# First block of the first MLP in two parts, with the second block between them; seven tiles of weights converted during the second block

## The chip, the cores and the metric

One core of a Trainium2 chip runs the whole kernel. The metric is the device time of one execution in microseconds (us). The matmul engine is TensorE (PE in the profile; PEld is its weight loads), VectorE is DVE, ScalarE is ACT, GpSimd is POOL, and SyncE (SP) issues all DMAs. TensorE's clock has two levels, 2.4 GHz and 1.2 GHz; the profile gives the granted share.

## The reference, cut to what matters

A linear attention with a decaying state feeds two MLPs, all in float32:

```python
# attention: q, k, v, alpha of shape (4, 8, 768, 48)
for t in range(S):
    state = alpha[:, :, t, :, None] * state + k[:, :, t] (outer) v[:, :, t]
    y[:, :, t] = q[:, :, t] @ state
x = y as (3072 tokens, 384)
h = x @ w1_in;  x1 = (h * sigmoid(1.702 * h)) @ w1_out      # d_ff 2048
h = x1 @ w2_in; out = (h - tanh(h)) @ w2_out                # d_ff 2048
```

## The kernel before

**MLPs.** The 3072 tokens are six blocks of 512 (`L1`, `L2`). A *step* is one block with one of 16 tiles `m` of 128 hidden units. `gemm1` makes the hidden tile (nine matmuls of 128x512: three parts of d_model times three products of high and low halves), `sig_1` the activation (ACT tanh at L387, then DVE at L388 into `gf`), `g_split` its high half on ACT (`ghi`, L391) and low half (`glo`, L392) on DVE or POOL, and `gemm2` (nine matmuls) adds the tile's share to three accumulator banks. `gemm2` runs `LAG = 3` steps behind `gemm1`. The hidden tile has two banks by turns (`HB[s % 2]`), so `gemm1` of step s waits for `sig_1` of step s-2. There are 192 steps; steps 0 to 15 are the first block, 16 to 31 the second. At the end of a block `evac` scales the banks into `xs` and stores them to `x1t` in DRAM.

**Weights** come as float64 and are converted by `conv`, which works on three tiles at a time: `w_split` of the oldest (`whi` on ACT at L191, `wlo` on DVE at L192), `w_join` of the next (DVE, L174), `w_bits` of a third (DVE, L161 and L162). Before the steps `conv` runs five times, which leaves tiles 0 to 2 done, 3 joined and 4 started; then it runs once in each step of the first block (13 of these 16 calls have work). The float buffers are three `cf` tiles and, for the first MLP, two more inside `xs`.

**Attention** goes by chunks g of 128 tokens, four to a block, six to a batch row; chunks 0 to 3 are done before step 0. The steps of a block make the next block's chunks: in the first block one chunk in three steps. A chunk's work: `prep(g, 0)` and `prep(g, 1)` are two scans (DVE, L241; the first with a reciprocal), `prep(g, 2)` two multiplications (L247, L248; DVE for chunks below 8, then POOL), `prep(g, 3)` is `a_guard` (ACT, L252), which squares the scans' results in place; `a_scores(g, 0)` and `a_scores(g, 1)` are matmuls (L277) into banks 5 and 6, copied out by ACT (L282, L290) and masked by POOL (L287) for chunks below 8; `a_out` makes the output (L306, L313) and the state's increment (L322); `a_state` (DVE, L333, L334) needs the scan of chunk g+1; `a_evac` copies the output out, `a_done` stores it, loads chunk g+2 and (`a_back`) brings the output back with d_model on the partitions; `a_x` splits it into `xhi` (ACT, L363) and `xlo`.

**Order.** From `begin` to the end of step 15, `in_order` chains the instructions of each engine's queue in the order in which the code issues them. An instruction there waits behind all that stands before it on its engine. After that a planner sets the order. The names above have their lines below; these few set the order inside a step of the first block:

```python
gemm1(i, m, h, n)
conv(1); fetch()                       # one tile further; its next load
g_split(*prev)
attend(4 + r // 4, r % 4)              # r by m: scores, scores, output
sig_1(s, h, n)
a_done, a_state at m % 3 == 2; prep(.., 3) a step later
gemm2(m, s - LAG, acc, n)
```

Of the kernel before, what the change touches and what calls it, by code (L numbers as in the profile page):

```python
# [17 lines left out]
C = 128  # L18
# [4 lines left out]
NP = H // 2  # L23
DP = 112
NB = 512
L1 = [(t, 512) for t in range(0, NTOK, 512)]
L2 = [(t, 512) for t in range(0, NTOK, 512)]
KT = DM // 128
# [40 lines left out]
def linear_attention_mlps(ctx, tc, xq, xv, fa, fv, cst, w1, w2, out):  # L69
# [49 lines left out]
    for _ in range(2):  # L119
# [22 lines left out]
    x1t = dr.tile([KT, 128, NTOK], F32, name="x1t")  # L142
    xt = dr.tile([H, D, NTOK], F32, name="xt")

    cfs = {
        1: cf + [xsf[:, i * WC : (i + 1) * WC] for i in range(2)],
        2: cf + f_c,
    }


    wsrc = {1: w1, 2: w2}
# [186 lines left out]
    def a_evac(g, b):  # L338
        ys = ysb[g % 2 if g < FULL else 0]
        for hh in range(2):  # L340
            A.copy(ys[:DP, 2 * C * hh : 2 * C * hh + 2 * C], bank[b + hh][:DP, : 2 * C])
        y4 = ys.rearrange("p (b a t) -> p b a t", b=2, a=2)
        tk = slice(g * C, g * C + C)
        for n in range(2):
            for hh in range(2):
                SP.dma_start(out=xt[2 * n + hh :: 4, :, tk].rearrange("h d t -> d h t"), in_=y4[64 * n : 64 * n + D, hh])  # L346
        if g >= FULL:
            a_back(g)
            a_x(g)


    def a_at(g):
        j = max(j for j, (t, _) in enumerate(L1) if t <= g * C)
        return xhi[j % 2], xlo[j % 2], slice(g * C - L1[j][0], g * C - L1[j][0] + C)

    def a_back(g):
        _, xl, o = a_at(g)
# [7 lines left out]


    def gemm1(i, m, h, n):
        xh, xl = xhi[i % 2], xlo[i % 2]
        c = 0
        for k in range(KT):  # L370
            ws = slice(k * 128, (k + 1) * 128)
            for w, x in ((whi, xh), (whi, xl), (wlo, xh)):
                P.matmul(out=h, lhsT=w[m][:, ws], rhs=x[:, k, :n], start=c == 0, stop=c == 3 * KT - 1)  # L373
                c += 1

    def gemm2(m, s, acc, n):
        for k in range(KT):
            ws = slice(DM + k * 128, DM + (k + 1) * 128)
            for c, (w, x) in enumerate(((whi, ghi), (wlo, ghi), (whi, glo))):
                P.matmul(out=acc[k][:, :n], lhsT=w[m][:, ws], rhs=x[s % 3][:, :n], start=m == 0 and c == 0,  # L380
                         stop=m == MT - 1 and c == 2)

    HB = [bank[3], bank[4]]

# [33 lines left out]
    def tanh_2(s):  # L418
        V.copy_predicated(gf[s % 2], f_m[0], f_d[0])

    def evac(l, t0, n, acc):
        for k in range(KT):
            if k == 1:
                V.tensor_scalar(out=xs[:, k, :n], in0=acc[k][:, :n], scalar1=0.5 if l == 1 else 1.0, scalar2=None,
                                op0=ALU.mult)
            else:
                A.activation(out=xs[:, k, :n], in_=acc[k][:, :n], func=AF.Copy, scale=0.5 if l == 1 else 1.0)
            if l == 2:
                SP.dma_start(out=out[k, :, t0 : t0 + n], in_=xs[:, k, :n])
        if l == 1:  # L430
            SP.dma_start(out=x1t[:, :, t0 : t0 + n].rearrange("k p t -> p k t"), in_=xs[:, :, :n])
# [3 lines left out]
        SP.dma_start(out=xr, in_=x1t[:, :, t0 : t0 + n].rearrange("k p t -> p k t"))  # L435

    def x1_split(j, k):
        i = (len(L1) + j) % 2
        A.copy(xhi[i][:, k], xr[:, k])  # L439
        G.tensor_tensor(out=xlo[i][:, k], in0=xr[:, k], in1=xhi[i][:, k].bitcast(F32), op=ALU.subtract)  # L440


    LAG = 3
# [113 lines left out]
    prep(4, 2)  # L557
    prep(4, 3)

    steps = [(1, j, m) for j in range(len(L1)) for m in range(MT)] + [(2, j, m) for j in range(len(L2)) for m in range(MT)]  # L560
    NS, NS1 = len(steps), len(L1) * MT

    def place(s):
# [2 lines left out]
        t0, n = (L1 if l == 1 else L2)[j]  # L566
        alt = i >= len(L1) - 1 and (i - len(L1)) % 2
        return l, j, m, i, t0, n, [bank[b] for b in ((5, 6, 7) if alt else (0, 1, 2))]

    for s in range(NS + LAG):  # L570
        if s:
# [3 lines left out]
        if s < NS:  # L575
            l, j, m, i, t0, n, acc = place(s)
            h = HB[s % 2][:, :n]
            gemm1(i, m, h, n)
            if l == 1 and j:
                sig_1(s, h, n)  # L580
            elif l == 1:
                conv(1)
                fetch()
            if l == 2:
# [3 lines left out]
        if s == NS:  # L588
            u_flag()
        if s < NS:  # L590
            if l == 1 and j + 1 < len(L1):
                t1, n1 = L1[j + 1]
                if j:
                    parts, span = n1 // C * 4, 11
                    todo = range(min(parts, -(-m * parts // span)), min(parts, -(-(m + 1) * parts // span)))
                else:
                    todo = ((4 * (m // 3) + m % 3,) if m % 3 < 2 else (4 * (m // 3) + 2, 4 * (m // 3) + 3)) if m < 12 else ()
                for r in todo:
                    attend(t1 // C + r // 4, r % 4)
            if l == 1 and j == 0:  # L600
                sig_1(s, h, n)
                if m % 3 == 2 and m < 12:
                    a_done(m // 3 + 4)
                    a_state(m // 3 + 4)
                if m % 3 == 0 and 0 < m < 13:
                    prep(m // 3 + 4, 3)
                if m % 3 == 1 and m > 3:
                    a_x(m // 3 + 3)
            if 2 <= j < 4 and m % 2:
                w_check(l, 8 * (j - 2) + m // 2)  # L610
            if 2 <= j < 4 and not m % 2:
# [22 lines left out]
                        x1_split(j + 1, m - 6)  # L634
        if s >= LAG:
            l, j, m, i, t0, n, acc = place(s - LAG)
            gemm2(m, s - LAG, acc, n)
            if m == MT - 1:
                evac(l, t0, n, acc)
        if s == MT - 1:  # L640
            in_order(begin)


# [103 lines left out]
```

## Time and profile before

| | us |
|---|---|
| median of 3 runs (lowest to highest) | 963.45 (963.1 to 965.75) |
| profiled execution, device time | 968.22 |
| its span, first to last instruction | 966.2 |
| TensorE busy in the span | 924.4 (96%) |
| DVE busy | 611.3 (63%) |
| ACT busy | 458.5 (47%) |
| POOL busy | 191.5 (20%) |

The span is what the trace covers; the device time has 2.0 us more around it. The profiled execution is 4.8 us longer than the median of the runs. Shares over the whole span mix stages: the 48 us before the first step, the first block, the blocks with attention beside them, and the rest.

### The profile page before, as it was taken

Reading aid. Unit: us, or ns where it says so; the run is one execution under the profiler, and the core shown is the slowest. Engines: PE = TensorE matmul, PEld = TensorE weight load, DVE = VectorE, ACT = ScalarE, POOL = GpSimd, SP = SyncE. Lnnn points to the kernel's source line nnn. Section 1 sums busy time; section 2 is a strip of 40 time slices with the busy share of each in tenths; the row PEclk is TensorE's granted clock in tenths of the full one; section 3 lists DMA queues with packets and bytes.
Section 4 is the critical chain, followed back from the end, with each engine's and each line's share of the span. In section 5 each row is a group of like instructions: output and inputs, shape, how many; then the busy total and the mean of one; then the engine's idle time right before and its main releaser. Section 6 shows DMA issues by size and latency. Waiting matters only on the chain.

```text
span 966.2 us, 13208 instructions
## 1 busy us (share of the span) xinstructions
PE 924.4 (96%) x4870; PEld 728.8 (75%) x4870; DVE 611.3 (63%) x916; ACT 458.5 (47%) x969; POOL 191.5 (20%) x150
## 2 busy tenths in 40 slices
PE   5579999999999999999999999999999999999997
PEld 4357777777777777777788888888888888888885
DVE  7799982442444453643249996776777777766663
ACT  4445534333444534333344564555555665545542
POOL 1201213453444444343320200100100101000000
PEclk9989999999999999999999999999999999999999
DMA  9767533231465443751224330100323430000001
GB/s 254 229 186 234 159 83 96 73 106 63 138 194 190 139 143 104 267 170 46 87 67 163 130 131 1 66 33 1 98 99 98 165 98 0 34 1 1 33 1 37
DMA packets 58042, 101.84 MB, mean 105 GB/s; under 512 B 4992, under 2 KB 37376, under 8 KB 57968
## 3 DMA queue, kind: packets, MB, share of 16 engines
q1 hardware_dynamic: 57968, 100.90, 33.1%
q8 instruction: 40, 0.66, 0.3%
q14 instruction: 34, 0.28, 0.1%
HBM read 86.73 MB, written 14.16 MB: 104 GB/s over the span
## 4 chain that ended last, share of the span: by engine, by line
PE 83%; DVE 7%; DMA 4%; issue 1%; ACT 1%; SPq 1%; POOL 0%; DVEq 0%; ACTq 0%
PE bank L380 38%; PE bank L373 38%; PE bank L277 3%; DMA arena<-xq 3%; PE bank L313 2%; DVE arena L241 2%; DVE wlo L192 1%; PE bank L306 1%; PE bank L322 1%; DVE glo L392 1%; SPq L346 1%; DVE cf L174 1%; DMA cs<-cst 1%; DVE gt L388 1%; DVE xs L174 0%
## 5 line engine op out<-in xcount | busy, mean ns | idle before, releaser
L373 PE MATMUL bank<-xhi,whi 128*128 128x512 f32 x576 | 230.8, 401 | 14.1 <-ACT xhi L363 8.6
L380 PE MATMUL bank<-ghi,whi 128*128 128x512 f32 x576 | 230.5, 400 | 0.0
L373 PE MATMUL bank<-xlo,whi 128*128 128x512 f32 x576 | 230.1, 399 | 0.0
L380 PE MATMUL bank<-ghi,wlo 128*128 128x512 f32 x576 | 229.5, 398 | 0.0
L373 PE MATMUL bank<-xhi,wlo 128*128 128x512 f32 x576 | 229.3, 398 | 0.0
L391 ACT CAST ghi<-gt 128x512 fp32r<-128x512 f32 x192 | 118.9, 619 | 227.1 <-DVE gt L403 123.8
L380 PE MATMUL bank<-glo,whi 128*128 128x512 f32 x576 | 225.6, 398 | 0.0
L373 PEld LDWEIGHTS bank<-xhi,whi 128*128 128x128 f32 x576 | 109.5, 190 | 41.8 <-ACT xhi L363 8.8
L392 DVE TENSOR_TENSOR glo<-gt,ghi 128x512 fp32r<-128x512 f32 x128 | 93.1, 727 | 74.3 <-ACT ghi L391 71.0
L388 DVE SCALAR_TENSOR_TENSOR gt<-gt,bank 128x512 f32<-128x512 f32 x96 | 65.3, 680 | 118.1 <-ACT gt L387 105.9
L380 PEld LDWEIGHTS bank<-ghi,whi 128*128 128x128 f32 x576 | 109.0, 189 | 27.3 <-issue 2.2
L373 PEld LDWEIGHTS bank<-xlo,whi 128*128 128x128 f32 x576 | 109.6, 190 | 26.6 <-issue 1.4
L373 PEld LDWEIGHTS bank<-xhi,wlo 128*128 128x128 f32 x576 | 109.4, 190 | 25.7 <-issue 0.6
L380 PEld LDWEIGHTS bank<-ghi,wlo 128*128 128x128 f32 x576 | 109.0, 189 | 25.5 <-issue 0.8
L380 PEld LDWEIGHTS bank<-glo,whi 128*128 128x128 f32 x576 | 109.0, 189 | 25.1
L392 POOL TENSOR_TENSOR glo<-gt,ghi 128x512 fp32r<-128x512 f32 x64 | 87.5, 1368 | 122.2 <-ACT ghi L391 111.3
L440 POOL TENSOR_TENSOR xlo<-arena,xhi 128x512 fp32r<-128x512 f32 x18 | 27.9, 1583 | 307.4 <-ACT xhi L439 307.4
L241 DVE TENSOR_TENSOR_SCAN arena<-arena,seg 112x516 f32<-112x516 f32 x46 | 64.0, 1390 | 35.3 <-DMA arena<-xq 34.2
L401 DVE SCALAR_TENSOR_TENSOR arena<-arena,bank 128x512 f32<-128x512 f32 x96 | 65.7, 685 | 30.4 <-ACT arena L399 29.7
L387 ACT ACTIVATE gt<-bank 128x512 f32<-128x512 f32 x96 | 57.4, 598 | 53.5 <-PE bank L373 53.5
L399 ACT ACTIVATE arena<-bank 128x512 f32<-128x512 f32 x96 | 57.3, 597 | 42.2 <-PE bank L373 41.8
L403 DVE SCALAR_TENSOR_TENSOR gt<-arena 128x512 f32<-128x512 f32 x96 | 68.2, 711 | 9.4
(86 smaller groups left out, 813.2 us busy)
## 6 DMA issues: line engine op xcount, KB each, us to landing
raw<-w SPq DMA_DIRECT2D x64, 768.0 KB, 4.6
arena<-xq SPq DMA_DIRECT2D x46, 224.0 KB, 3.0
arena<-xq SPq DMA_DIRECT2D x22, 451.5 KB, 5.6
xlo<-xt SPq DMA_DIRECT2D x24, 192.0 KB, 4.3
x1t<-xs SPq DMA_DIRECT2D x6, 768.0 KB, 5.2
arena<-x1t SPq DMA_DIRECT2D x6, 768.0 KB, 4.5
out<-xs SPq DMA_DIRECT2D x18, 256.0 KB, 2.3
arena<-xv SPq DMA_DIRECT2D x23, 192.0 KB, 2.8
```

The lines of the kernel that those rows point to most:

```text
L241: V.tensor_tensor_scan(out=dec(g, n), data0=src(g, n), data1=seg, initial=0.0, op0=ALU.mult, op1=ALU.max)
L277: P.matmul(out=o[hh][:, i], lhsT=k[r, 2 * x + i], rhs=q[r, 2 * x + i], start=True, stop=True)
L373: P.matmul(out=h, lhsT=w[m][:, ws], rhs=x[:, k, :n], start=c == 0, stop=c == 3 * KT - 1)
L380: P.matmul(out=acc[k][:, :n], lhsT=w[m][:, ws], rhs=x[s % 3][:, :n], start=m == 0 and c == 0, stop=m == MT - 1 and c == 2)
L387: A.activation(out=th[i][:, :n], in_=h, func=AF.Tanh, scale=0.851)
L388: V.scalar_tensor_tensor(out=gf[i][:, :n], in0=th[i][:, :n], scalar=1.0, in1=h, op0=ALU.add, op1=ALU.mult)
L391: A.copy(ghi[s % 3][:, :n], gf[s % 2][:, :n])
L392: e.tensor_tensor(out=glo[s % 3][:, :n], in0=gf[s % 2][:, :n], in1=ghi[s % 3][:, :n].bitcast(F32), op=ALU.subtract)
L399: A.activation(out=u, in_=h, func=AF.Square, accum_out=usum[:, s - NS1 :][:, :1])
L401: V.scalar_tensor_tensor(out=p, in0=u, scalar=P3, in1=h, op0=ALU.mult, op1=ALU.mult)
L403: V.scalar_tensor_tensor(out=gf[i], in0=w, scalar=PD, in1=p, op0=ALU.add, op1=ALU.mult)
L440: G.tensor_tensor(out=xlo[i][:, k], in0=xr[:, k], in1=xhi[i][:, k].bitcast(F32), op=ALU.subtract)
```

## The change

The steps of the first MLP get a new order: nine steps of block 0, all sixteen of block 1, the last seven of block 0, then blocks 2 to 5 as before. So the four chunks of block 1 must be ready after nine steps instead of sixteen; a table, `HALVES`, says which pieces of attention go into which half of each of these nine steps. Conversion runs in six of the nine steps (tiles 3 to 8) and in eight steps of block 1 (tiles 9 to 15), with three float buffers. The chunks of block 2 are made from the seventh step of block 1 on and brought back in one go after it, since block 1 and block 2 now use the same `xhi`, `xlo` buffers. Block 0's accumulators are stored after its ninth step, read back later, and the second part is added to them on DVE. The written order ends at step 14.

```diff
+SPLIT = 9
-        1: cf + [xsf[:, i * WC : (i + 1) * WC] for i in range(2)],
+    cfs = {1: cf, 2: cf + f_c}
+    def xb(i):
+        i += i > 1
+        return xhi[i % 2], xlo[i % 2]
...
-        if g >= FULL:
+        if g >= FULL + 4:
             a_back(g)
             a_x(g)
...
-    def gemm2(m, s, acc, n):
+    def gemm2(m, s, acc, n, first=0, last=MT - 1):
...
-    def evac(l, t0, n, acc):
+    def evac(l, t0, n, acc, more=False):
         for k in range(KT):
-            if k == 1:
+            if more:
+                V.scalar_tensor_tensor(out=xs[:, k, :n], in0=acc[k][:, :n], scalar=0.5, in1=xs[:, k, :n], op0=ALU.mult, op1=ALU.add)
+            elif k == 1:
...
-    steps = [(1, j, m) for j in range(len(L1)) for m in range(MT)] + [(2, j, m) for j in range(len(L2)) for m in range(MT)]
+    steps = [(1, 0, m) for m in range(SPLIT)] + [(1, 1, m) for m in range(MT)] + [(1, 0, m) for m in range(SPLIT, MT)]
+    steps += [(1, j, m) for j in range(2, len(L1)) for m in range(MT)] + [(2, j, m) for j in range(len(L2)) for m in range(MT)]
...
+    HALVES = ("", "P50 S4", "P51 T4", "O4 P52", "D4 S5", "T5", "O5 P60 P61", "P62 D5 S6", "T6 P70", "O6 P71 X4",
+              "P72 D6 S7", "T7 X5", "O7", "D7 X6", "", "", "X7", "")
+
+    def half(t):
+        for what in HALVES[t].split():
+            g = int(what[1])
+            if what[0] == "P":
+                prep(g, int(what[2]))
+            if what[0] in "ST":
+                a_scores(g, what[0] == "T", 5)
+            if what[0] == "O":
+                a_out(g, 5)
+            if what[0] == "D":
+                a_done(g)
+                if g + 1 < FULL:
+                    a_state(g)
+                    prep(g + 1, 3)
+            if what[0] == "X":
+                a_x(g)
...
             gemm1(i, m, h, n)
-            if l == 1 and j:
+            if l == 1 and (j > 1 or not j and m >= SPLIT):
                 sig_1(s, h, n)
-            elif l == 1:
+            elif l == 1 and (m in (0, 1, 2, 3, 5, 7) if j == 0 else m % 3 < 2 and m < 11):
                 conv(1)
                 fetch()
...
+            if l == 1 and (j == 1 and m >= 6 or j == 0 and m == SPLIT):
+                t = m - 6 if j else 10
+                if t == 0:
+                    for r in range(3):
+                        prep(FULL, r)
+                    a_state(FULL - 1)
+                    prep(FULL, 3)
+                for r in range(-(-t * 16 // 11), -(-(t + 1) * 16 // 11)):
+                    attend(FULL + r // 4, r % 4)
+            if l == 1 and j == 0 and m >= SPLIT:
+                t = m - SPLIT
+                if t == 0:
+                    for g in range(FULL, FULL + 4):
+                        a_back(g)
+                        a_x(g)
+                if t == 4:
+                    SP.dma_start(out=xs, in_=x1t[:, :, t0 : t0 + n].rearrange("k p t -> p k t"))
...
-            if l == 1 and j == 0:
+            if l == 1 and j == 0 and m < SPLIT:
+                half(2 * m)
+            if l == 1 and (j == 1 or not j and m < SPLIT):
                 sig_1(s, h, n)
...
         if s >= LAG:
             l, j, m, i, t0, n, acc = place(s - LAG)
-            gemm2(m, s - LAG, acc, n)
-            if m == MT - 1:
-                evac(l, t0, n, acc)
-        if s == MT - 1:
+            parted = l == 1 and j == 0
+            gemm2(m, s - LAG, acc, n, SPLIT if parted and m >= SPLIT else 0, SPLIT - 1 if parted and m < SPLIT else MT - 1)
+            if m == MT - 1 or parted and m == SPLIT - 1:
+                evac(l, t0, n, acc, parted and m == MT - 1)
+        if s < SPLIT:
+            half(2 * s + 1)
+        if s == SPLIT + 5:
             in_order(begin)
```

In `HALVES` P52 is `prep(5, 2)`, S and T are the two halves of a chunk's scores, O is `a_out`, D is `a_done` with `a_state` and the next chunk's guard, X is `a_x`. The even entries stand between `g_split` and `sig_1` of a step, the odd ones behind its `gemm2`.

## Rows read from the trace of the kernel before

**Rows 1.** Steps 0 to 15 and 16 to 31: length, busy us (instructions), clock, DMA.

```profile
48.41:142.75 94.34, 83.30 (x485) 62.90 (x486) 88.28 (x125) 43.73 (x99) 16.31 (x12) 0.95 0.57 169
142.75:226.42 83.67, 83.67 (x529) 64.65 (x528) 32.29 (x57) 31.76 (x71) 34.96 (x27) 1.00 0.32 92
```

**Rows 2.** Waits of TensorE, 142.75 to 425 us: total, times, longest.

```profile
PE bank L306 <- ACT arena L290: 0.2, 1, 0.2
```

**Rows 3.** Chain of waits: start, us, what; one full-speed group of nine matmuls.

```profile
153.58 2.10 PE bank L373 x9
```

**Rows 4.** DVE in order of time, first block: start, us, instruction, [idle before].

```profile
59.25 0.06 DVE L240 MEMSET seg<- 112x4 f32 x1
...
72.84 0.35 DVE L333 TENSOR_TENSOR state<-bank,state 112x192 f32<-112x192 f32 x1
...
73.50 0.95 DVE L192 TENSOR_TENSOR wlo<-cf,whi 128x768 fp32r<-128x768 f32 x1
...
77.02 0.68 DVE L392 TENSOR_TENSOR glo<-gt,ghi 128x512 fp32r<-128x512 f32 x1
...
79.11 0.66 DVE L388 SCALAR_TENSOR_TENSOR gt<-gt,bank 128x512 f32<-128x512 f32 x1
79.68 0.95 DVE L192 TENSOR_TENSOR wlo<-cf,whi 128x768 fp32r<-128x768 f32 x1
...
83.20 0.68 DVE L392 TENSOR_TENSOR glo<-gt,ghi 128x512 fp32r<-128x512 f32 x1
83.80 1.22 DVE L241 TENSOR_TENSOR_SCAN arena<-arena,seg 112x516 f32<-112x516 f32 x1
84.94 0.66 DVE L388 SCALAR_TENSOR_TENSOR gt<-gt,bank 128x512 f32<-128x512 f32 x1
...
85.99 0.95 DVE L192 TENSOR_TENSOR wlo<-xs,whi 128x768 fp32r<-128x768 f32 x1
...
89.79 0.69 DVE L247 TENSOR_TENSOR arena<-arena 112x512 f32<-112x512 f32 x1
...
90.99 0.68 DVE L388 SCALAR_TENSOR_TENSOR gt<-gt,bank 128x512 f32<-128x512 f32 x1
...
119.64 1.66 DVE L392 TENSOR_TENSOR glo<-gt,ghi 128x512 fp32r<-128x512 f32 x1
```

**Rows 5.** ACT in order of time, first and second block.

```profile
53.66 1.06 ACT L252 ACTIVATE arena<-arena 112x1032 f32<-112x1032 f32 x1 [4.56 <-DVE arena L248]
...
69.09 0.84 ACT L191 CAST whi<-cf 128x768 fp32r<-128x768 f32 x1
...
79.86 0.62 ACT L391 CAST ghi<-gt 128x512 fp32r<-128x512 f32 x1 [3.19 <-DVE gt L388]
80.38 0.64 ACT L282 COPY arena<-bank 128x256 f32<-128x256 f32 x2
...
81.17 0.63 ACT L387 ACTIVATE gt<-bank 128x512 f32<-128x512 f32 x1
...
177.94 1.07 ACT L252 ACTIVATE arena<-arena 112x1032 f32<-112x1032 f32 x1 [0.53 <-DVE state L334]
...
205.45 0.51 ACT L363 CAST xhi<-xlo 128x384 fp32r<-128x384 f32 x1 [4.67 <-DMA xlo<-xt]
```

**Rows 6.** POOL in order of time, first block.

```profile
62.69 0.90 POOL L287 TENSOR_SCALAR_AFFINE_SELECT arena<-arena 128x512 f32<-128x512 f32 x1 [5.67 <-ACT arena L282]
...
118.87 1.88 POOL L247 TENSOR_TENSOR arena<-arena 112x512 f32<-112x512 f32 x1
```

**Rows 7.** TensorE in order of time, step 2.

```profile
61.42 0.79 PE L373 MATMUL bank<-xhi,whi 128*128 128x512 f32 x1 [3.80 <-DVE gt L388]
```

**Rows 8.** One stretch, columns as in Rows 1; the clock is the third last.

```profile
60.10:67.00 6.90, 5.58 (x29) 3.90 (x31) 6.83 (x10) 2.67 (x7) 0.90 (x1) 0.51 0.52 186
```

**Rows 9.** DMA issues: count, KB each, median us to landing.

```profile
arena<-xq SPq DMA_DIRECT2D x22, 451.5 KB, 5.6
xlo<-xt SPq DMA_DIRECT2D x24, 192.0 KB, 4.3
```

More of the change, by code (lines that the diff above doesn't have):

```diff
@@ L143, in linear_attention_mlps @@
     xt = dr.tile([H, D, NTOK], F32, name="xt")
-    cfs = {
-        1: cf + [xsf[:, i * WC : (i + 1) * WC] for i in range(2)],
-        2: cf + f_c,
-    }
+    cfs = {1: cf, 2: cf + f_c}
+    def xb(i):
+        i += i > 1
+        return xhi[i % 2], xlo[i % 2]
     wsrc = {1: w1, 2: w2}
@@ L353, in a_at @@
         j = max(j for j, (t, _) in enumerate(L1) if t <= g * C)
-        return xhi[j % 2], xlo[j % 2], slice(g * C - L1[j][0], g * C - L1[j][0] + C)
+        return *xb(j), slice(g * C - L1[j][0], g * C - L1[j][0] + C)
     def a_back(g):
@@ L367, in gemm1 @@
     def gemm1(i, m, h, n):
-        xh, xl = xhi[i % 2], xlo[i % 2]
+        xh, xl = xb(i)
         c = 0
@@ L379, in gemm2 @@
             for c, (w, x) in enumerate(((whi, ghi), (wlo, ghi), (whi, glo))):
-                P.matmul(out=acc[k][:, :n], lhsT=w[m][:, ws], rhs=x[s % 3][:, :n], start=m == 0 and c == 0,
-                         stop=m == MT - 1 and c == 2)
+                P.matmul(out=acc[k][:, :n], lhsT=w[m][:, ws], rhs=x[s % 3][:, :n], start=m == first and c == 0,
+                         stop=m == last and c == 2)
     HB = [bank[3], bank[4]]
@@ L437, in x1_split @@
     def x1_split(j, k):
-        i = (len(L1) + j) % 2
-        A.copy(xhi[i][:, k], xr[:, k])
-        G.tensor_tensor(out=xlo[i][:, k], in0=xr[:, k], in1=xhi[i][:, k].bitcast(F32), op=ALU.subtract)
+        xh, xl = xb(len(L1) + j)
+        A.copy(xh[:, k], xr[:, k])
+        G.tensor_tensor(out=xl[:, k], in0=xr[:, k], in1=xh[:, k].bitcast(F32), op=ALU.subtract)
     LAG = 3
@@ L590, in linear_attention_mlps @@
         if s < NS:
-            if l == 1 and j + 1 < len(L1):
-                t1, n1 = L1[j + 1]
[L593 to L598, printed above, removed]
+            if l == 1 and (j == 1 and m >= 6 or j == 0 and m == SPLIT):
[15 more added lines that the diff above has]
+                    SP.dma_start(out=xs, in_=x1t[:, :, t0 : t0 + n].rearrange("k p t -> p k t"))
+            if l == 1 and 1 < j and j + 1 < len(L1):
+                t1, n1 = L1[j + 1]
+                parts, span = n1 // C * 4, 11
+                for r in range(min(parts, -(-m * parts // span)), min(parts, -(-(m + 1) * parts // span))):
                     attend(t1 // C + r // 4, r % 4)
-            if l == 1 and j == 0:
+            if l == 1 and j == 0 and m < SPLIT:
+                half(2 * m)
+            if l == 1 and (j == 1 or not j and m < SPLIT):
                 sig_1(s, h, n)
[L602 to L608, printed above, removed]
             if 2 <= j < 4 and m % 2:
```

## The prediction

> **What bounds the kernel now.** I read the table by stretches first, one stretch for each block of 16 steps. From step 16 on TensorE has no idle time: steps 16 to 31 take 83.67 us and TensorE is busy for all of them [rows 1], and the list of waits has 0.2 us for it up to 425 us [rows 2]. A group of nine matmuls at full speed takes 2.10 us [rows 3], so the 32 groups of these steps are 67.2 us and the four chunks beside them 16.5, 4.1 a chunk (by the order of its matmuls about 1.0 for each half of the scores and 2.1 for the output with the state's increment; 1.0 to 1.6 for the output of a first or last chunk of a row). Steps 0 to 15 hold three groups less, since the second GEMM runs three steps behind: 83.67 - 6.3 = 77.4 us of TensorE. They take 94.34. So 17 us are lost in the first block, and nothing that this change touches can win more.
>
> Next I asked who makes TensorE wait there. DVE is busy for 88.28 of the 94.34 us [rows 1]; in order of time its instructions stand back to back. One step's share, from start to start [rows 4]: conversion 3.52 (73.50 to 77.02, and 79.68 to 83.20 again), `glo` and a first scan with its reciprocal 2.09 (77.02 to 79.11), of which `glo` is 0.60 (83.20 to 83.80), so that scan is 1.49; second scan 1.14 (83.80 to 84.94); the activation's product 0.57 (79.11 to 79.68); product and `xlo` 1.05 (84.94 to 85.99), so `xlo` 0.48; two multiplications 1.20 (89.79 to 90.99); state 0.66 (72.84 to 73.50). In step 2 TensorE waited 3.80 us for the product of step 0 [rows 7] and then ran at 0.51 of its clock, the 1.2 GHz level [rows 8].
>
> **What leaves the first part, and what doesn't.** Seven conversions, 7 x 3.52 = 24.6 us of DVE, go from the first block into the second, with their loads; of the first nine steps three lose theirs (4, 6 and 8), and steps 0 to 3 keep one each. The scans of chunks 5 to 7 stood in the first nine steps before, too; but the scores and outputs of four chunks now stand in seven steps instead of twelve, each ahead of the next step's `gemm1` in TensorE's queue. Everything up to step 14 runs in the written order, so I add the queues up from the last point that both orders share: DVE at 59.25, done with step 0's conversion [rows 4]. ACT and POOL prices: `ghi` 0.52 (79.86 to 80.38), copies of one half of the scores 0.79 (80.38 to 81.17), tanh 0.6, `whi` 0.84, guard 1.06 [rows 5], mask 0.9 [rows 6].
>
> *Link 1, output of chunk 4 before step 2.* O4 now stands ahead of `gemm1` of step 2, and needs the mask of T4. Product of step 0 ends 59.8, `ghi` 60.4, copies and mask: O4 at about 62, where `gemm1` started at 61.42 before. The idle time is much the same (some 4 us), and so is the slow clock behind it: O4 to 66, `gemm1` of step 2 to 68.5, S5 to 69.6. DVE meanwhile: scan 61.3, conversion 64.8, `glo` and scan 66.5, product 67.1, P52 68.3, conversion 71.8, `glo` 72.4, state 73.1.
>
> *Link 2, the guard.* `a_guard` overwrites the scans' results in place, so it waits for whoever reads them: for the multiplications (4.56 us at 53.66) and for the state (0.53 at 177.94) [rows 5]. Before, the guard stood a step behind the state. Now D4 puts guard 5 in ACT's queue right behind the state of chunk 4, which DVE does at 73.1, behind a conversion. ACT stands from about 68 to 73.1, and behind the guard are S5's copies (guard 74.2, copies 75.0), which T5 waits for on TensorE with `gemm1` of step 3 behind it, and the tanh of step 2, which DVE waits for. TensorE idles about 5 us; T5 at half clock to 77.0, its copies 77.8, `whi` of tile 6 78.6. Only then DVE goes on with step 3's conversion; since 73.1 it has done one product in 5.5 us.
>
> *Link 3, chunk 6.* DVE: conversion 82.1, `glo` and first scan 84.2, second scan 85.3, product 85.9, P62 87.1. TensorE: step 3's `gemm1` 79.3, O5 80.9, `gemm2` 83.0; then S6, with `gemm1` of step 4 behind it, waits until 87.1: 4.1 us. The chunk's load, issued about 72 and landing in 5.6 [rows 9], is in time.
>
> *Link 4, chunk 7.* S6 (partly slow) 88.5, copies 89.3, `ghi` 89.8, `glo` 90.4, first scan 91.9. `gemm1` of step 4 at the slow clock 91.9, T6 92.9, copies 93.7, tanh 94.3, product 94.9, second scan 96.0, `xlo` 96.5, conversion 100.0, `glo` 100.6, P72 101.8. TensorE is done with `gemm2`, O6 and `gemm1` of step 5 at 98.1 and waits 3.7 us for S7.
>
> *Link 5, to the start of step 16.* Nothing is late any more: conversion and product are 4.1 us a step in two steps of three against 4.2 of TensorE. Left are S7, T7, O7 (4.1), ten first and eleven second GEMM groups (21 x 2.10 = 44.1) and about 1.5 for a slow clock behind the last gap: 101.8 + 49.7 = 151.5. In the trace of before the same work is done at 142.75. **The front costs 8.7 us.**
>
> The slow clock in it, from T5 on, is an estimate by step 2's pattern (a gap of 3.80, then the low level): 1.0 for T5, 0.3 for step 3, 0.4 and 1.3 for S6 and step 4, 1.5 at the end, 4.5 in all; if the clock holds, the front costs 4.2.
>
> **The other edits, with both bounds.**
> - Conversion in block 1: DVE is busy 32.29 of 83.67 us there [rows 1], and 24.6 more fit: 0. Against it: POOL makes `glo` in this block, and a DVE subtraction took 1.66 us instead of 0.60 while POOL's multiplication ran from 118.87 to 120.75 [rows 4, 6]. With 1.1 us on each step, two steps of three take 5.2, and 1.0 us a step piles up that the third works off: at most 2.
> - The Trainium skill says of this (SBUF — State Buffer, section "SBUF: two separate sides") that a DVE instruction with two SBUF inputs and a GpSimd instruction exclude each other for a whole instruction. The row agrees in kind: 1.06 us of the 1.88 were waited out. By the rule alone each step of block 1 could lose up to one whole POOL instruction, so the rule speaks against moving work there; the sum would be up to 2 us higher.
> - Bringing block 2's chunks back in one go: ACT splits them behind four DMAs of 4.3 us [rows 9]. A wait of 4.67 on the same splitting in block 1 cost TensorE nothing [rows 5, 2]: 0. At worst the store of chunk 11, its two DMA landings and a load's issues make it some 10 us, of which two steps (8.4) less the activation's 2.5 are covered: 4.
> - Three buffers for five: five calls leave tile 4 started with either, since a buffer is free when its split is done: 0. One more evacuation, store and load on idle queues: 0. The evacuation with an addition puts three DVE products of 0.66 on one queue, the next `gemm1` (2.10) covers them: 0, at most 1.4.
> - Blocks 2 to 5, and the second MLP: the same work, TensorE-bound: 0.
>
> The sum is made against the profiled execution: 968.22 + 8.7 = 976.9. Its own 4.8 us over the median are the same for both, so on the median it is 963.45 + 8.7 = 972.
>
> **The rivals.** A measurement of this kernel tells 0.3%, 2.9 us, from no change.
> - *The guard costs nothing* (0.17): link 2 goes, if ACT reaches the guard late anyway or DVE has the state done early. Then chunk 6's multiplications end 4.9 us earlier and the front costs 3.8, or 0.6 with a clock that holds (4.5 less the 1.3 of T5 and step 3): 964 to 967. For it: one guard in the trace waited 0.53 only; against it: the state stands behind a conversion of 3.52 in DVE's written order.
> - *DVE's relief decides, faster* (0.17): DVE bounds the front, 24.6 us of it leave, and TensorE runs through from S6. With S6 at 82.2, the scores and outputs of chunks 6 and 7 (7.1) and 24 groups (50.4) end at 139.7: 3.0 us gained, 960.4. It needs chunk 7's multiplications by the end of step 5's first GEMM, 3.7 us sooner than link 4, no slow clock and no wait for the guard. For it: 88.28 of 94.34 us. Against it: the four conversions that stay are the four that were in the way.
> - *The seam costs as well* (0.09): the return of block 2's chunks and the contention of DVE and POOL, 4 to 8 us on top: 976 to 980.
> - The forecast (0.57): 967.5 with a clock that holds, to 976 with the three waits (12.8 us) a third longer.
>
> **How the numbers follow.** The likeliest is 972; its own range is 967.5 to 976. To leave out no more than 2 in 10, the range takes in most of the first rival and the seam, and leaves out the faster case and the far end: 963 to 978. Slower by over 0.3%: 0.57 + 0.09 and 0.04 of the first rival, 0.70; the same: 0.13 and 0.02 of the faster one, 0.15; faster 0.15.
>
> **What would show it.** Right: step 16 (the 145th to 153rd matmul of the first GEMM) starts near 151; in the first nine steps three idle times of 3.5 to 5 us end at matmuls of the scores (L277), one of them behind a guard (L252) on ACT that waits about 5 us for the state (L334), the other two behind DVE's multiplications (L248); the granted clock falls behind them; DVE's busy time in block 1 rises by about 24 us and TensorE has no idle time there. Wrong: step 16 before 143, DVE without idle time in the first nine steps, or idle time of TensorE where the first block's second part begins.

## The result, and the profile after

| us | before | after |
|---|---|---|
| median (lowest to highest of 10 runs each) | 963.61 (962.63 to 971.37) | 976.64 (973.6 to 979.14) |
| profiled execution, its span | 968.22, 966.2 | 976.9, 974.9 |

The ratio is 1.0118, 95% interval 1.01 to 1.0137: 1.2% slower. 972 was predicted, with a range of 963 to 978.

Where the time went is read from the starts of the steps (step s starts with matmul 9s + 1 of the first GEMM). At step 48 both kernels have done the same work: three whole blocks and the chunks up to 11.

| start, us | step 0 | 2 | 3 | 4 | 5 | 6 | 9 | 16 | 48 | 64 | 80 |
|---|---|---|---|---|---|---|---|---|---|---|---|
| before | 48.41 | 61.42 | 68.12 | 76.78 | 82.15 | 88.12 | 105.11 | 142.75 | 311.01 | 395.44 | 483.79 |
| after | 47.65 | 63.32 | 75.74 | 87.47 | 96.46 | 107.24 | 124.20 | 157.18 | 322.36 | 406.36 | 492.41 |

The lag, after's start less before's, is 19.1 us at step 9. After has then done four chunks, before only about three; the lag settles at 11.35 by step 48, and it comes from the front alone (steps 0 to 8 and what they leave to the queues). Step 0 itself starts 0.76 us sooner in after, with the same work ahead of it, so from step 0 to step 48 after takes 12.1 us longer. First the windows of after: steps 0 to 15, the part of block 1 up to step 24, and the seven steps of block 0 behind it.

```profile
47.65:157.18 109.53, 91.50 (x518) 68.29 (x518) 88.87 (x122) 46.26 (x105) 23.17 (x18) 0.89 0.52 154
...
124.20:206.65 82.45, 82.45 (x482) 62.67 (x481) 49.45 (x73) 33.56 (x66) 32.82 (x22) 1.00 0.32 94
206.65:239.76 33.11, 33.11 (x176) 25.87 (x175) 17.81 (x29) 13.28 (x29) 9.19 (x7) 1.00 0.37 120
```

Against [rows 1], TensorE's idle time in steps 0 to 15 is 18.0 us instead of 11.0, and DVE, with 88.87 us against 88.28 in a stretch 15 us longer, now has gaps. From step 9 on TensorE is busy the whole time: neither the seven conversions in block 1 nor the seam (steps 25 to 31) costs it a wait. The waits themselves are these, TensorE in order of time, with the idle time before each instruction in brackets; they answer to [rows 7].

```profile
60.52 0.79 PE L311 MATMUL bank<-arena,state 48*48 48x128 f32 x16 [3.52 <-ACT arena L295]
67.86 0.87 PE L282 MATMUL bank<-arena 48*128 48x176 f32 x8 [1.34 <-ACT arena L346]
74.13 1.68 PE L282 MATMUL bank<-arena 48*128 48x176 f32 x8 [5.41 <-ACT arena L295]
86.00 1.54 PE L282 MATMUL bank<-arena 48*128 48x176 f32 x8 [2.63 <-issue]
101.81 0.87 PE L282 MATMUL bank<-arena 48*128 48x176 f32 x8 [2.99 <-issue]
111.82 0.64 PE L318 MATMUL bank<-arena 128*48 128x128 f32 x8 [1.07 <-POOL arena L292]
```

They are O4, S5, T5, S6, S7 and O7. Scores and outputs of the attention, which came one chunk in three steps, now stand one behind the other in TensorE's queue, each with a `gemm1` behind it. ACT and DVE in order of time say who is late (line numbers of after are 5 higher: L257 is the guard, L339 and L341 the state, L253 the second multiplication, L246 the scan).

```profile
72.25 1.06 ACT L257 ACTIVATE arena<-arena 112x1032 f32<-112x1032 f32 x1 [4.50 <-DVE state L339]
...
73.83 0.39 ACT L295 COPY arena<-bank 128x96 f32<-128x96 f32 x2
74.09 0.63 ACT L392 ACTIVATE gt<-bank 128x512 f32<-128x512 f32 x1
...
85.93 1.06 ACT L257 ACTIVATE arena<-arena 112x1032 f32<-112x1032 f32 x1 [4.38 <-DVE arena L253]
...
102.01 1.06 ACT L257 ACTIVATE arena<-arena 112x1032 f32<-112x1032 f32 x1 [5.36 <-DVE state L341]
```

```profile
71.86 0.36 DVE L339 TENSOR_TENSOR state<-state,arena 112x192 f32<-112x192 f32 x1
74.75 0.69 DVE L393 SCALAR_TENSOR_TENSOR gt<-gt,bank 128x512 f32<-128x512 f32 x1 [2.54 <-ACT gt L392]
77.46 0.96 DVE L197 TENSOR_TENSOR wlo<-cf,whi 128x768 fp32r<-128x768 f32 x1 [2.02 <-ACT whi L196]
...
85.22 0.68 DVE L253 TENSOR_TENSOR arena<-arena 112x512 f32<-112x512 f32 x1
89.08 0.69 DVE L397 TENSOR_TENSOR glo<-gt,ghi 128x512 fp32r<-128x512 f32 x1 [3.18 <-ACT ghi L396]
...
94.42 0.69 DVE L393 SCALAR_TENSOR_TENSOR gt<-gt,bank 128x512 f32<-128x512 f32 x1 [3.15 <-ACT gt L392]
...
96.17 0.53 DVE L369 TENSOR_TENSOR xlo<-xlo,xhi 128x384 fp32r<-128x384 f32 x1
...
105.99 1.23 DVE L246 TENSOR_TENSOR_SCAN arena<-arena,seg 112x516 f32<-112x516 f32 x1 [4.02 <-DMA arena<-xq]
...
109.71 1.55 DVE L369 TENSOR_TENSOR xlo<-xlo,xhi 128x384 fp32r<-128x384 f32 x1
```

The three engines wait for each other in turn. DVE's state ends at 72.2, the guard starts, and behind the guard stand S5's copies, the last at 73.83, and the tanh at 74.09: T5 starts at 74.13, DVE's product at 74.75. DVE's multiplications end at 85.9: the second guard, and S6 at 86.00. S7 at 101.81 again starts behind the multiplications, and the third guard behind the state. The clock follows: it is at the 1.2 GHz level (0.51 in the third last column of the windows) around T5, in whose stretch TensorE had just been idle for 5.41 us, and again from S6 on.

```profile
72.00:79.00 7.00, 4.87 (x16) 3.85 (x17) 2.45 (x4) 4.65 (x13) 1.27 (x2) 0.51 0.97 281
85.60:92.50 6.90, 6.50 (x23) 4.82 (x25) 2.42 (x5) 2.60 (x7) 0.64 (x1) 0.51 0.50 144
```

All in all the low level held for 20.5 us of the front, from 61.7, 72.0, 85.6 and 102.7; before, for 10.2 of it. Step 0 is left out of both: its matmuls start 0.43 us apart in either kernel, those of step 1 0.23 apart; but before's profile has no record of the clock ahead of 53.3, so the 0.95 and 0.89 of the first windows don't compare. The DVE row at 105.99 is of another kind: it is a scan of chunk 8, which the code issues in step 15 only. The planner put it into the stretch where the written order holds, and there it waits 4.02 us for its load, ahead of step 5's product. TensorE doesn't wait for that product; what the early work of chunk 8 costs it shows by POOL, in order of time.

```profile
107.31 1.20 POOL L252 TENSOR_TENSOR arena<-arena 112x512 f32<-112x512 f32 x1 [2.85 <-DVE arena L246]
109.68 1.18 POOL L253 TENSOR_TENSOR arena<-arena 112x512 f32<-112x512 f32 x1 [1.17 <-DVE arena L246]
110.81 0.96 POOL L292 TENSOR_SCALAR_AFFINE_SELECT arena<-arena 128x512 f32<-128x512 f32 x1
```

Chunk 8's multiplications stand ahead of T7's mask (110.81), and O7 waits 1.07 us for that mask.

### The profile page after: what moved, and what is told of

Read it like the earlier page. It is cut to its first block, busy times and chain, and to the rows that moved or that the text cites. A ratio compares the mean times of both kernels' runs of the same rounds, so it can differ in the third digit from the quotient of the medians.

```text
span 974.9 us, 13225 instructions
## 1 busy us (share of the span) xinstructions
PE 926.6 (95%) x4870; PEld 730.9 (75%) x4870; DVE 619.1 (64%) x919; ACT 461.3 (47%) x969; POOL 192.1 (20%) x150
## 4 chain that ended last, share of the span: by engine, by line
PE 86%; DVE 4%; DMA 4%; issue 1%; ACT 1%; SPq 1%; POOL 1%; DVEq 0%; ACTq 0%; POOLq 0%
PE bank L385 40%; PE bank L378 39%; PE bank L282 4%; PE bank L318 2%; DMA raw<-w 1%; PE bank L311 1%; DMA arena<-xq 1%; DVE arena L246 1%; DVE cf L179 1%; PE bank L327 1%; DMA xlo<-xt 1%; POOL arena L292 1%; DMA cs<-cst 1%; SPq L351 1%; DVE wlo L197 1%
## 5 line engine op out<-in xcount | busy, mean ns | idle before, releaser
L397 POOL TENSOR_TENSOR glo<-gt,ghi 128x512 fp32r<-128x512 f32 x64 | 92.9, 1451 | 121.8 <-ACT ghi L396 106.9
L246 DVE TENSOR_TENSOR_SCAN arena<-arena,seg 112x516 f32<-112x516 f32 x46 | 63.6, 1383 | 39.4 <-DMA arena<-xq 38.4
```

The costliest lines, as they stand in the source:

```text
L246: V.tensor_tensor_scan(out=dec(g, n), data0=src(g, n), data1=seg, initial=0.0, op0=ALU.mult, op1=ALU.max)
L397: e.tensor_tensor(out=glo[s % 3][:, :n], in0=gf[s % 2][:, :n], in1=ghi[s % 3][:, :n].bitcast(F32), op=ALU.subtract)
```

## The experiments

All medians, ratios and starts in one table; every ratio is against runs of the kernel before on the same chip. Those had medians of 963.61 (beside after), 964.92 (e1, e2, e4, e6), 965.08 (e5, e7, e8, e9) and 965.57 (e10, e11), so a difference of two medians from different groups is good to one or two us only. Step 0 starts between 45.76 and 48.41 in the profiled executions; the last column is the time from step 0 to step 48, the same work in every kernel but for what e4_fill adds.

| kernel | median, us | ratio, 95% interval | step 0 | 3 | 4 | 5 | 6 | 9 | 14 | 48 | 0 to 48 |
|---|---|---|---|---|---|---|---|---|---|---|---|
| before | 963.61 | | 48.41 | 68.12 | 76.78 | 82.15 | 88.12 | 105.11 | 133.34 | 311.01 | 262.60 |
| after | 976.64 | 1.0118 (1.01 to 1.0137) | 47.65 | 75.74 | 87.47 | 96.46 | 107.24 | 124.20 | 148.26 | 322.36 | 274.71 |
| e1_guard | 975.17 | 1.011 (1.0089 to 1.0131) | 45.76 | 68.98 | 82.64 | 90.61 | 103.36 | 119.97 | 143.88 | 318.48 | 272.72 |
| e2_conv_end | 976.23 | 1.012 (1.0101 to 1.014) | 46.94 | 71.53 | 82.99 | 90.90 | 98.43 | 119.01 | 148.42 | 321.74 | 274.80 |
| e5_order | 959.84 | 0.9946 (0.9931 to 0.9962) | 46.47 | 62.49 | 69.46 | 76.82 | 85.95 | 103.77 | 130.19 | 303.72 | 257.25 |
| e10_order_conv_back | 970.67 | 1.0055 (1.0031 to 1.0079) | 46.63 | 69.54 | 77.49 | 84.69 | 95.43 | 117.09 | 141.27 | 315.29 | 268.66 |
| e11_order_guard_back | 968.99 | 1.0032 (1.0014 to 1.005) | 46.34 | 61.96 | 72.61 | 80.05 | 94.28 | 112.89 | 139.19 | 314.03 | 267.69 |
| e9_keep8_only | 981.11 | 1.0175 (1.0153 to 1.0198) | 46.70 | | | | | 121.24 | 142.15 | 325.39 | 278.69 |
| e7_keep8 | 975.91 | 1.0121 (1.0096 to 1.0146) | 47.86 | | | | 100.56 | 116.36 | 137.74 | 324.60 | 276.74 |
| e8_order_keep | 964.99 | 0.9999 (0.9985 to 1.0012) | 46.76 | | | | | 103.10 | 124.47 | 308.80 | 262.04 |
| e4_fill | 980.38 | 1.0164 (1.014 to 1.0188) | 47.02 | | | | | 125.75 | | 323.75 | 276.73 |
| e6_glo_dve | 975.21 | 1.0105 (1.0084 to 1.0126) | 47.22 | | | | | 123.70 | | 321.38 | 274.16 |

**The guard moved (e1_guard).** Guards 5, 6 and 7 go behind the scores' second half of their own chunk.

```diff
-    "T5"
+    "T5 G5"
...
-    "T6 P70"
+    "T6 G6 P70"
...
-    "T7 X5"
+    "T7 G7 X5"
...
-                    prep(g + 1, 3)
+            if what[0] == "G":
+                prep(g, 3)
```

> The changed kernel with one edit: the guards of chunks 5, 6 and 7 are issued behind the second half of the same chunk's scores, no longer directly behind the state. Theory of the prediction (three separate waits in the front, the guard's worth 4.9 us): 4 to 5 us less than the changed kernel, about 972 us, T5 starts some 5 us sooner and step 16 as much. Second form of it (the waits are in a row, and DVE's multiplications for chunk 6 come next): T5 sooner by 4 to 5 us, but the wait before S6 grows, and step 16 comes only 1 to 2 us sooner. Rival (the seam and the second block cost, not the front): no change.

TensorE's waits for T5, S6 and S7 (the rows of after at 74.13, 86.00 and 101.81):

```profile
67.73 1.31 PE L282 MATMUL bank<-arena 48*128 48x176 f32 x8 [0.90 <-ACT arena L295]
81.17 1.54 PE L282 MATMUL bank<-arena 48*128 48x176 f32 x8 [4.71 <-issue]
97.00 1.54 PE L282 MATMUL bank<-arena 48*128 48x176 f32 x8 [4.03 <-issue]
```

T5's wait falls from 5.41 to 0.90, but those for S6 and S7 grow by 2.08 and 1.04. (S5's, ahead of the moved guard, grows from 1.34 to 2.89 while O4's falls from 3.52 to 2.01; counted from step 0 both start where they do in after.) Of the 3.9 us by which step 48 starts sooner, 1.9 are already there at step 0 (45.76), so the front gains 2.0 in this execution; the median falls by 1.5, and the intervals of the two ratios overlap. That is the second form of the expectation. The guard's wait is real and stands ahead of others nearly as long.

**Conversions at the end of the step (e2_conv_end).** In steps 0, 1, 2, 3 and 5 `conv(1); fetch()` goes from behind `gemm1` to the end of the step.

```diff
-            elif l == 1 and (m in (0, 1, 2, 3, 5, 7) if j == 0 else m % 3 < 2 and m < 11):
+            elif l == 1 and (m == 7 if j == 0 else m % 3 < 2 and m < 11):
...
             half(2 * s + 1)
+            if s in (0, 1, 2, 3, 5):
+                conv(1)
+                fetch()
```

> The changed kernel with one edit: the conversions of steps 0, 1, 2, 3 and 5 are issued at the end of the step, behind the product and the pieces of attention, instead of ahead of them; the same work in each step. Theory (in the front TensorE waits for DVE's attention work that stands behind conversions in its queue): the waits before O4, S6 and S7 become shorter by 2 to 3 us each, 6 to 8 us less than the changed kernel, about 969. Rival (DVE is simply full, its order does not matter): no change, since DVE does the same work in the same steps. Rival (seam and second block): no change.

The 6 to 8 us that were expected don't come. O4's, S6's and S7's waits fall to 0.93, 2.31 and 1.29 us, but T5's, behind the guard, is the same as in after (the first line). Step 6 starts 8.8 us sooner than in after, and by step 14 nothing of it is left. TensorE, DVE and ACT in order of time show where it goes:

```profile
69.92 1.68 PE L282 MATMUL bank<-arena 48*128 48x176 f32 x8 [5.41 <-ACT arena L295]
...
104.23 0.64 PE L318 MATMUL bank<-arena 128*48 128x128 f32 x8 [2.27 <-POOL arena L292]
```

```profile
98.42 1.23 DVE L246 TENSOR_TENSOR_SCAN arena<-arena,seg 112x516 f32<-112x516 f32 x1 [3.71 <-DMA arena<-xq]
...
113.56 1.23 DVE L246 TENSOR_TENSOR_SCAN arena<-arena,seg 112x516 f32<-112x516 f32 x1 [1.84 <-DMA arena<-xq]
```

```profile
117.93 0.62 ACT L396 CAST ghi<-gt 128x512 fp32r<-128x512 f32 x1 [4.97 <-DVE seg L248]
```

The planner put scans of chunks 8 and 9 into the written order's stretch, where DVE stands 3.71 and 1.84 us for their loads, and the activation's chain stands behind DVE. TensorE waits 2.27 us at O7 for the mask, 1.26 at step 9 for `xhi`, and runs at the low level from 119.7 to 126.5.

**Chunk 8 held back (e9_keep8_only in after, e7_keep8 in e2_conv_end).** The memset that begins chunk 8's scan is kept at its place in the program.

```diff
-            V.memset(first, 1.0)
+            op = V.memset(first, 1.0)
+            if g == FULL:
+                tc.keep_in_program_order(op)
```

> The changed kernel with that one edit alone: chunk 8's first scan held at its written place. If the early scans cost in the front of the changed kernel too (one waits 4.0 us at 106 us with the product of step 5 queued behind it): step 9 1 to 3 us sooner and the kernel 1 to 3 us faster, about 974. If they only fill idle time: no change, or slower by up to 3 us because the chunks of block 2 start later.

> The kernel with conversions at the end of the step (e2_conv_end), and chunk 8's first scan instruction held at its written place, so that the planner can't set chunk 8's and 9's attention into DVE's and ACT's queues of steps 5 to 14. If the 8.8 us by which e2_conv_end led the changed kernel at step 6 were lost to these early instructions (its scan there waits 3.7 us for a load with a product queued behind it): step 9 near 115, step 14 near 136 instead of 148, and the kernel 5 to 8 us faster than e2_conv_end, about 969 us. If they were lost to something else (the return of chunk 7's output, the conversions of block 1): step 14 as before, near 148, no change in time, or slower since chunk 8 starts later.

Neither gain comes, though the expected starts do (116.36 and 137.74 in e7_keep8). Step 9 of e9_keep8_only starts 3.0 us sooner than in after (2.0 counted from step 0), and step 14 of e7_keep8 10.7 sooner than that of e2_conv_end. Of this O7's wait for the mask (1.07 in after, 2.27 in e2_conv_end) is the early scan's price; but by step 14 the kernels that hold chunk 8 back have also not done its scores and the first part of its output, 2.0 us of TensorE between after and e9_keep8_only and 6.3 between e2_conv_end and e7_keep8. That work comes back later, and with it waits of TensorE in steps 17 and 18, where after has none (e9_keep8_only, lines 2 higher again than in after; e7_keep8 has the same three):

```profile
157.84 0.50 PE L380 MATMUL bank<-xhi,whi 128*128 128x512 f32 x1 [0.89 <-DVE seg L245]
...
162.58 0.50 PE L380 MATMUL bank<-xhi,whi 128*128 128x512 f32 x1 [1.38 <-DVE gt L395]
...
168.38 1.20 PE L284 MATMUL bank<-arena 48*128 48x176 f32 x8 [1.35 <-ACT arena L297]
```

Step 48 starts 3.0 later than in after, and the median is 4.5 us above after's; e7_keep8 ends where e2_conv_end does (975.91 and 976.23). So the hoisted scan is not what makes after slow: taken as a whole, the early start of chunk 8 gains in after and changes nothing in e2_conv_end.

**The clock held by matmuls whose results nobody reads (e4_fill).** 20, 32, 16 and 18 more matmuls of 128x320 ahead of O4, T5, S6 and S7.

```diff
+    FILL = {"O4": 20, "T5": 32, "S6": 16, "S7": 18}
+    def fill(n):
+        for _ in range(n):
+            P.matmul(out=bank[7][:, 192:512], lhsT=whi[0][:, :128], rhs=xhi[0][:, 0, :320], start=True, stop=True)
...
+            fill(FILL.get(what, 0))
```

> The changed kernel with 86 added matmuls of 128x320 whose results nobody reads, in four places of the front, ahead of O4 (20), T5 (32), S6 (16) and S7 (18), where TensorE waits; nothing else. At full clock they take 2.3 to 4.6 us in each place, a little less than the waits. If the slow clock behind the waits is a cost of its own: the granted clock stays high in the front and the kernel is 3 to 5 us faster than the changed one in spite of the added work, about 973. If the clock costs nothing because TensorE then only waits longer at the next place: no change, or slower by what the added matmuls overhang, 0 to 3 us.

The low level holds for 10.2 us instead of 20.5, and the time rises by 3.7, against the 3 to 5 less that were expected if the slow clock were a cost of its own. Two of the groups of matmuls, TensorE in order of time:

```profile
71.25 6.38 PE L587 MATMUL bank<-xhi,whi 128*128 128x320 f32 x32 [2.79 <-DVE state L338]
...
101.86 4.37 PE L587 MATMUL bank<-xhi,whi 128*128 128x320 f32 x18 [3.21 <-DVE state L341]
```

They themselves waited for the state, which reads the bank that they write, and so ran past the wait that they were to fill: T5 starts at 77.56 instead of 74.13 and S7's first half at 106.16 instead of 101.81. In between the delay is made good (step 5 starts at 96.30, in after at 96.46), and at step 9 1.55 us are left. The trace prices both sides. Added up from start to start, without idle time, the kernel's own matmuls from step 0 to step 48 take 248.1 us instead of 256.7, and 4.5 us of them fall on the low level instead of 21.7. So the slow clock is a cost of its own: the faster one gives some 8.6 us back. TensorE's idle time falls from 18.0 to 12.3 us, but the added matmuls take 16.3, so idle and added time together are 10.6 us more. In these sizes and in this bank the filling costs more than it gives; shorter groups in a bank that no other engine reads were not tried.

**`glo` of block 1 on DVE (e6_glo_dve).** POOL no longer works beside DVE's conversions there.

```diff
-                prev = s - 1, n, V if l == 2 or j in (0, len(L1) - 1) else G
+                prev = s - 1, n, V if l == 2 or j in (0, 1, len(L1) - 1) else G
```

> The changed kernel with one edit: the low halves glo of block 1 are made by DVE instead of POOL, which takes POOL out of the steps in which the seven tiles are converted. If contention of POOL and DVE in these steps costs: 1 to 2 us less than the changed kernel. Theory of the front: TensorE has no idle time in block 1, so within 1 us of the changed kernel, either way; DVE gets 16 x 0.6 = 10 us more work there and has room for it.

Step 48 starts 1.0 us sooner, of which 0.5 are there at step 9, and the interval of its ratio and that of after overlap. The contention of DVE and POOL, which the prediction bounded by 2 us, is hidden behind TensorE.

**The same operations in another order (e5_order).** Same split, same conversions in the front, same attention pieces; the guards come behind their own chunk's second scores or output, the first scans early, and each conversion (C) at a place where the next scores don't wait for it.

```diff
-    HALVES = ("", "P50 S4", "P51 T4", "O4 P52", "D4 S5", "T5", "O5 P60 P61", "P62 D5 S6", "T6 P70", "O6 P71 X4",
-              "P72 D6 S7", "T7 X5", "O7", "D7 X6", "", "", "X7", "")
+    HALVES = ("", "P50 S4 P51", "P52", "T4 C", "O4 D4 S5", "C", "T5 P60 P61 G5", "O5 D5 P62", "C", "P70 S6 T6",
+              "P71 P72 O6 G6 C D6", "X4 S7 C T7", "O7 G7", "D7 X5 X6", "C", "X7", "", "")
...
+            if what == "C":
+                conv(1)
+                fetch()
+                continue
...
-                    prep(g + 1, 3)
+            if what[0] == "G":
+                prep(g, 3)
...
-            elif l == 1 and (m in (0, 1, 2, 3, 5, 7) if j == 0 else m % 3 < 2 and m < 11):
+            elif l == 1 and (False if j == 0 else m % 3 < 2 and m < 11):
```

> The changed split, 9 + 16 + 7 steps, with another order inside the nine steps: the same scans, multiplications, scores, outputs, guards and six conversions, placed so that by adding up the queues no score waits for DVE; scans of chunk 7 ahead of scores of chunk 6, guards off the way, the last conversion in the seventh step. By the addition step 4 starts near 71 (87 in the changed kernel), step 9 near 101 (124), step 14 near 122 (148). If the order of the front is the whole cost, the kernel is faster than the one before by 5 to 10 us, 954 to 959. If the planner's early instructions of chunks 8 and 9 eat a part, step 14 near 130 and 960 to 966. Rival (the seam or the second block cost): slower than before still, 970 or more.

> e5_order with chunk 8's first scan held at its written place. If the planner's early instructions cost: faster than e5_order by 2 to 6 us, step 14 near 122 to 126, 952 to 958 us. If they fill idle time: equal to e5_order or slower by up to 4 us, since in this order TensorE has little idle time left and chunk 8 comes later.

It beats both kernels: 0.54% below before, 1.7% below after, between the 954 to 959 expected if the order is the whole cost and the 960 to 966 if chunk 8's early instructions eat a part. Steps 0 to 15 in its windows:

```profile
46.47:139.36 92.89, 89.22 (x532) 66.14 (x532) 87.65 (x122) 46.03 (x104) 26.69 (x19) 0.98 0.61 185
```

DVE's work is the same 122 instructions (87.65 us against 88.87 in after), TensorE's idle time is 3.7 us instead of 18.0, and the longest wait that it has in the steps is 0.90. e8_order_keep, the same with chunk 8 held back, is 5.2 us slower, a little more than the 4 that its second form allowed: again step 14 sooner (124.47, with 4.8 us less of chunk 8's matmuls done), step 48 later, and TensorE's idle time up to there 9.1 us instead of 3.7.

**Either part of that order undone (e10_order_conv_back, e11_order_guard_back).** One puts the six conversions back behind `gemm1`, the other the guards back into D. In the second the guard of chunk 6 comes ahead of the multiplications that read what it squares, which changes that chunk's values; the work is the same.

```diff
e10_order_conv_back
-    "T4 C", "C", "C", "P71 P72 O6 G6 C D6", "X4 S7 C T7", "C"
+    "T4", "", "", "P71 P72 O6 G6 D6", "X4 S7 T7", ""
...
-            elif l == 1 and (False if j == 0 else m % 3 < 2 and m < 11):
+            elif l == 1 and (m in (0, 1, 2, 3, 5, 7) if j == 0 else m % 3 < 2 and m < 11):
e11_order_guard_back
-    "T5 P60 P61 G5", "P71 P72 O6 G6 C D6", "O7 G7"
+    "T5 P60 P61", "P71 P72 O6 C D6", "O7"
...
-            if what[0] == "G":
-                prep(g, 3)
+                    prep(g + 1, 3)
```

> The reordered kernel (959.84 us, 0.9946 of the time before), with one part of its order undone: its six conversions stand directly behind the first GEMM of steps 0, 1, 2, 3, 5 and 7 again, ahead of the split and the activation's product, and the attention's pieces keep the new order. If the place of the conversions is one of the two things that the order is worth: adding up the queues, chunk 5's scores wait about 3.7 us near 69 and chunk 7's about 3 us near 94 again, step 9 starts some 11 us later than in the reordered kernel (103.8, so about 115), and if that lasts the time is 968 to 972. If the conversions' place alone is worth nothing, as moving it alone was (976.23 against 976.64): step 9 within 3 us of 103.8 and 959 to 962. If the planner gives the lag back behind the written order, as it gave back a lead: step 9 late, step 48 within 2 us of 303.7 and 959 to 962.

> The reordered kernel (959.84 us) with the other part undone: the guard of the next chunk stands right behind the state again, in D, and the conversions keep their new places. If the guard's place costs what stands behind it on ACT (the copies of the next scores) once nothing else is late: adding up the queues, the second half of chunk 5's scores waits about 1.9 us near 68, the second half of chunk 7's about 4.6 near 93.5, step 9 some 8 to 10 us later than 103.8 and 966 to 970. If the guard is worth no more here than it was by itself in the changed kernel (1.5 us, 975.17 against 976.64): step 9 at 105 to 106 and 960 to 962.

TensorE's waits in the first of them, then TensorE's and ACT's in the second:

```profile
58.17 0.80 PE L378 MATMUL bank<-xhi,whi 128*128 128x512 f32 x1 [2.19 <-DVE seg L245]
67.89 1.73 PE L282 MATMUL bank<-arena 48*128 48x176 f32 x8 [3.91 <-ACT arena L346]
...
92.72 0.87 PE L282 MATMUL bank<-arena 48*128 48x176 f32 x8 [2.03 <-issue]
```

```profile
66.30 1.00 PE L282 MATMUL bank<-arena 48*128 48x176 f32 x8 [1.98 <-ACT arena L295]
...
92.67 1.68 PE L282 MATMUL bank<-arena 48*128 48x176 f32 x8 [5.32 <-ACT arena L295]
```

```profile
89.89 1.06 ACT L257 ACTIVATE arena<-arena 112x1032 f32<-112x1032 f32 x1 [5.98 <-DVE state L341]
```

Both first expectations come out: step 9 is 13.3 and 9.1 us later than in e5_order, the medians 10.8 and 9.2 us higher (10.5 and 8.3 by the ratios). The waits stand where they were expected, in the second also in size; in the first the one at 92.72 is 2.03 instead of about 3, and two that were not expected, 2.19 at 58.17 and 2.06 for O7's mask at 102.55, make up for it. And by themselves the moved conversions and the moved guard gave after only 0.4 and 1.5 us, neither clear of noise. These are waits in a row: while one of the two stands, the other's going gains little. The early scans, the third thing that e5_order changed, were not put back by themselves, so their share is not shown. The loss was not made up behind the written order: step 48 is still 11.6 and 10.3 us later.

## Why the prediction was right, and by how much its sum was off

**The mechanism was right.** The places and lengths of the waits, with the prediction's own in brackets: O4 at 60.52 after 3.52 us (62, some 4); T5 at 74.13 after 5.41 (75.0, about 5), behind a guard that waits 4.50 for the state (5.1); S6 at 86.00 after 2.63 (87.1, 4.1); S7 at 101.81 after 2.99 (101.8, 3.7). Line L339 stands where the prediction has L334, and the clock fell in or behind each. That S7 comes out to the hundredth is luck. S6's and S7's waits are shorter than expected; S5's 1.34 was not expected; step 0 starts 0.76 us sooner; and the slow clock's term was too small. TensorE is busy for 14.5 us of the low stretches from 72.0 on (4.7, 6.5 and 3.4), and a first-GEMM matmul there takes 0.43 us from start to start instead of 0.23, so 6 to 7 us are lost, an estimate from these rows, where the prediction has 4.5. e5_order, e10 and e11 show that this order is the cause: with the same split and work, the front alone decides between 959.84 and 976.64.

**The sum was too small: link 5.** "8.7 us" came from 49.7 us between S7 and step 16. At equal work, by step 48, after is 11.35 behind, so 2.6 more, and as S7 itself is on time all of it comes after S7. (Counted from step 0, the front costs 12.1; the other 0.8 lie before S7.) Of the 2.6, O7's 1.07 for the mask is seen; "nothing is late any more" overlooked chunk 8's scan and multiplications, which the planner moved into the written order. The other 1.5 lie in the price of the groups. Added up from start to start, without idle time, the 21 GEMM groups between S7 and step 16 take 47.3 us, where link 5 has 44.1 and 1.5 for the slow clock. The slow clock's part fits (seven matmuls, 2.98 us instead of about 1.6); the rest take 2.19 us a group, not the 2.10 of a group by itself in [rows 3]; in steps 16 to 47 of before they average 2.17. That step 16 itself starts at 157.18, not 151.5, is for 3.1 of these 5.7 us chunk 8's scores and part of its output done early, which come back later (the lag falls from 14.4 at step 16 to 11.35).

**The spans agree by accident.** 974.9 - 966.2 = 8.7 is the predicted figure, but before's profiled execution has a wait in block 4 that this execution of after lacks:

```profile
426.98 1.19 PE L277 MATMUL bank<-arena 48*128 48x176 f32 x8 [1.18 <-ACT arena L290]
```

with the low clock behind it (428.8 to 432.2); the lag falls there, from 10.92 at step 64 to 8.62 at step 80. Other kernels have it too (e10_order_conv_back 1.54 us at 431.2). The medians differ by 13.0. That is the 12.1 from step 0 to step 48 and 0.9 that one profile of each can't place.

**The other edits.** Zero was right: no wait of TensorE from 112 us on is longer than 0.4 us.

```profile
PE bank L318 <- POOL arena L292: 1.1, 1, 1.1
PE bank L282 <- ACT arena L295: 0.4, 1, 0.4
```

(The first of these two ends at 111.82.) Contention is there, as [rows 4, 6] had it: DVE's `xlo` at 109.71 took 1.55 us instead of 0.53 (at 96.17) beside POOL's multiplication of 1.18 from 109.68. The rule of the Trainium skill (SBUF — State Buffer, section "SBUF: two separate sides") that the two exclude each other for a whole instruction is borne out by this pair too, 1.02 of the 1.18. It cost TensorE nothing in block 1 (e6_glo_dve). DVE's busy time there is 49.45 us, a rise of 17 on [rows 1] and not of 24, since some of the chunks' work left the block (7 scans instead of 8, 12 multiplications of scores instead of 16) and two of the seven tiles were begun in the front.

**The rivals.** *The guard costs nothing* fell: it waited 4.50. But its price was wrong, too: taking the wait away was to give 4.9 us and more with the clock, and it gave 1.5. Counted from step 0, T5 starts 4.5 us sooner in e1_guard, but "chunk 6's multiplications end 4.9 us earlier" came to 2.9: step 3's conversion, which stands ahead of them on DVE, still waits for `whi`, and the scores still wait for DVE. What TensorE gains at T5 is partly waited out again at S6 and S7. *DVE's relief decides* was refused on "the four conversions that stay are the four that were in the way". That holds for the places that the change gives them. Placed otherwise, they are not in the way, and the gain that the rival priced at 3.0 us is 5.2 (965.08 to 959.84) in e5_order. *The seam costs as well* came near the measured time for another reason: the seam has no wait.

## What to carry to other kernels

When chunks of work are packed into fewer steps, write the new order by what each in-order queue holds ahead of the next matmul, not by the order in which the pieces are thought of: here the same 122 DVE instructions cost TensorE 18.0 or 3.7 us of waiting. Undo suspects from the good version, not only from the bad one: waits in a row hide each other (0.4 and 1.5 us, within noise, removed singly; 10.8 and 9.2 us put back singly). An operation in place (the guard) waits for all readers of what it overwrites, and everything behind it in its queue waits too, so it belongs behind the last thing that somebody is waiting for.

## What the runs showed that was not expected

- Matmuls added to keep the clock up took the low level from 20.5 to 10.2 us of the front, and the kernel became 3.7 us slower: they and the idle time that was left took 10.6 us more of TensorE than the idle time before, and the clock gave back 8.6.
- A scan that the planner moved some 44 us ahead (105.99, against 149.80 where it is held) stood 4.02 us for a DMA in the ordered stretch, and yet holding it back lost 4.5 us: TensorE then waits three times, 3.6 us together, in steps where after has no wait.
